# One gate and one lead of a planned order: attention and a feed-forward stage on one core

## The chip, the cores and the metric

The kernel runs on one core of a Trainium2 chip. A core has five engines that run beside each other, each through its own list of instructions: TensorE (PE in the profile, with PEld for its weight loads), VectorE (DVE), ScalarE (ACT), GpSimd (POOL) and SyncE (SP, which here only issues DMAs). They wait for each other by semaphores. The metric is the device time of one execution in microseconds.

## The reference

Eight batches of attention whose 12 heads are mixed twice, and then a feed-forward stage with a squared ReLU:

```python
batch, n_heads, seq, head_dim = (8, 12, 448, 64)
scores = scale * np.matmul(q, k.transpose(0, 1, 3, 2))
scores = np.einsum('bhij,hg->bgij', scores, w_pre)
scores = scores - np.max(scores, axis=-1, keepdims=True)
attn = np.exp(scores)
attn = attn / (np.sum(attn, axis=-1, keepdims=True) + 1e-09)
attn = np.einsum('bhij,hg->bgij', attn, w_post)
return np.matmul(attn, v).astype(np.float32)
...
x = np.ascontiguousarray(attn_out.transpose(0, 2, 1, 3)).reshape(B * S, H * D)
h = np.maximum(x @ w_in, 0.0)          # x: 3584 x 768, w_in: 768 x 2048
return (h * h @ w_out).astype(np.float32)
```

## The kernel before

Batches are counted from 0 to 7. A batch's 448 queries fall into 45 chunks of mostly 10 queries (`NCHUNK`, `CI`), and the chunks into four blocks (`C0 = [0, 6, 19, 32]`). The work of a batch:

- Loads by GpSimd (`load_q`, `load_kv`, `load_tail`): `qs`, `ks`, `vs`, `qt`. Queries and keys come in two halves of six heads.
- Turning queries and keys: in batches 0 and 1 on TensorE against an identity (`t_qk`, L618; `t_tail`, L646); from batch 2 on by copies on GpSimd (`x_piece`, L682) and transposing DMAs on SyncE (L695 for keys, L701 for queries, L665 for the tail).
- `score` (L763): queries times keys, per block. The result is evicted from PSUM to `snat` by VectorE (L556) or ScalarE (L558).
- `relayout` (L794): a DMA on SyncE that gathers a chunk's 10 queries of all 12 heads from `snat` into one tile `sch` of 120 rows. There are 14 `sch` tiles.
- Mixing the heads before the softmax: one matmul with `wmix` (L923), or, for two chunks at once, eight quarter-array matmuls (`mix_two`, L869; 60 or 64 rows and columns). Fourteen chunks of batch 0 take another way, without a relayout (L929).
- The softmax of a chunk: minimum on VectorE (L934), exponential with the sum on ScalarE (L937), the reciprocal of two chunks' sums at once on VectorE (L944), and the scaling of the second mixing weights by these on GpSimd (L947, "weight scaling", one per chunk, so two wait for the same reciprocal).
- The second mixing (L954: four matmuls), eviction to `atb`, and the product with `vs` in half-array matmuls (`av`, L1000), evicted to `xt`.
- The feed-forward stage in units of 128 or 256 columns of `xt` (`unit`): L1059 (`w_in`), ReLU to `hr` on VectorE (L1073) or ScalarE (L1077), square to `h` on GpSimd (L1080), L1098 (`w_out`), eviction to `osb`, store (L1122).

The order in which each engine gets its instructions is not written by hand. A `Planner` gets every operation with its engines, a duration, a rank (`pri`) and what it depends on, runs through them on a clock of its own, and at each moment takes the ready operation of least rank on each engine. What it takes is emitted, in that order; the chip runs these lists as they stand. Rank counts in chunks: chunk `n` of batch `b` has `n = b * NCHUNK + place`. The mix has rank `n`, the weight scaling `n + 0.5`, the second mixing `n + 1.5`; feed-forward work has ranks of a million and more, so it fills what attention leaves. The planner also puts idle filler matmuls (L1323, tile `still`) where it sees TensorE idle in the first 130 us.

What the change touches: `AHEAD` is the lead of a relayout over its chunk,

```python
pri = n - AHEAD                                                                  # L808, relayout
pri = n - o % (2 * PAIRS) + 0.1 * (o % (2 * PAIRS)) - AHEAD                      # L828, in pairs
pri = b * NCHUNK + first - AHEAD - 0.6 - (0.7 if r == 0 else 1.4) * (NPAIR - p)  # L768, score
```

and `Q1_AT` says behind which places of batch 0 the two halves of batch 1's queries and keys are loaded. `load_ahead(1, n, ...)` gives them the rank `n + LATER` (`LATER = 2`), and `gate(n)` makes them depend on the weight scaling of place `n`. The planner lets an operation on the same engine go 70 ns behind a weight scaling's end (`lat=70` at L983).

Of the kernel before, what the change touches and what calls it, by code (L numbers as in the profile page):

```python
# [40 lines left out]
PIECE = NPAIR // 2  # L41
NE = 6
NSCH = 14
AHEAD = 7.5
FIFO = 50
IDLE_NS, IDLE_COLS, IDLE_FROM, IDLE_END, IDLE_LOW = 112, 256, 1300, 130000, 0.62
SPELL, PHASE, DROP, RISE = 3413, 1700, 0.4, 0.8
# [38 lines left out]
NEAR_AT = 5  # L86
SOON = 0
W2_AT = [14, 17, 20, 23]
Q1_AT = [9, 11]
W1_AT = [0, 1, 2, 3, 4, 5]  # L90
W1_GATE = 0
TAIL0, Q0 = 19, 0.7
# [270 lines left out]
def kernel(  # L363
# [370 lines left out]
    def place_of(b, c):  # L734
        return b * NCHUNK + (ORDER0.index(c) if b == 0 else c)
# [6 lines left out]
    def is_direct(b, c):  # L742
        return b == 0 and C0[1] <= c <= C0[2]
# [5 lines left out]
    def score(b, r, group):  # L749
# [17 lines left out]
        first = min(place_of(b, c) for c in range(C0[r], (C0 + [NCHUNK])[r + 1]) if not is_direct(b, c)) - b * NCHUNK  # L767
        pri = b * NCHUNK + first - AHEAD - 0.6 - (0.7 if r == 0 else 1.4) * (NPAIR - p)  # L768
        n = b * (NJ + 1) + r - 2
# [30 lines left out]
    def relayout(b, c):  # L800
# [6 lines left out]
        deps = list(scopy[b, r]) + (list(scopy[b, r - 1]) if r == 1 and cc == 0 else [])  # L807
        pri = n - AHEAD  # L808
        if r == 2 and cc == 0:
# [15 lines left out]
        else:  # L825
            o = cc - 1
            if b >= PAIR_FROM:
                pri = n - o % (2 * PAIRS) + 0.1 * (o % (2 * PAIRS)) - AHEAD  # L828
            o, step = (2 * CI * (o // 2) + o % 2, 2) if b >= PAIR_FROM else (o, CPR)
# [376 lines left out]
    def load_w2(f4, n):  # L1206
        f_, c_ = 8 * (f4 % 2), 384 * (f4 // 2)
        done = load(64, (62, 79), n, lambda: nc.gpsimd.dma_start(
            out=w2[:, f_:f_ + 8, c_:c_ + 384],
            in_=moe_w_out[128 * f_:128 * f_ + 1024, c_:c_ + 384].rearrange("(f p) c -> p f c", p=128),  # L1210
        ), gate(n))
        done.next.append(w2_in[f4])
        w2_in[f4].left += 1
# [8 lines left out]
    def load_ahead(b, n, g0):  # L1222
        wars = [op for p in range(g0 // 2, g0 // 2 + 3) for op in got_op[b - 1, p]]
        got = [
            load(48, (36, 52), n + LATER, lambda: load_q(b, g0, g0 + 6), wars + gate(n)),
            load(42, (46, 58), n + LATER, lambda: load_kv(ks, k, b, g0, g0 + 6), wars + gate(n)),
        ]
        if g0 == 0:
            load_tails(b, n + LATER, got_tail[b - 1] + gate(n))
        later[b, g0] = add("BOTH", 0, n, lambda: None, got, lat=0)  # L1230

    def first_batch():
# [7 lines left out]
        for n, c in enumerate(ORDER0):  # L1240
# [12 lines left out]
            if n in W2_AT:  # L1253
                load_w2(W2_AT.index(n), n)
            if n in Q1_AT:
                load_ahead(1, n, 6 * Q1_AT.index(n))
            if c == C0[1]:
# [106 lines left out]
```

## Time and profile before

| | |
|---|---|
| median of 3 runs | 568.91 us (567.85 to 569.1) |
| the profiled execution | 569.35 us |
| its span in the profile | 567.6 us |
| TensorE busy | 558.4 us, 98% |
| VectorE busy | 500.7 us, 88% |
| ScalarE busy | 446.9 us, 79% |
| GpSimd busy | 363.4 us, 64% |
| read from and written to HBM | 45.61 MB, 11.01 MB |

The span is the profiled execution from its first to its last instruction; the time of the execution is 1.75 us longer. Busy shares are shares of the span. A row of a timeline gives the start in us, the length in us, engine, line, operation, tile written and tiles read, and the number of instructions joined; in brackets stands the idle time before it and what ended it. A matmul's recorded length contains its way through the array, so neighbours overlap, and what one costs is read from start to start.

### The profile page before, as it was taken

What the parts mean: (1) busy time and instruction counts of PE and PEld (TensorE: products, weight loads), DVE (VectorE), ACT (ScalarE), POOL (GpSimd) and SP (SyncE); (2) the same over time, 40 slices, a digit from 0 to 9 for tenths busy, and PEclk for the clock granted to TensorE, in tenths of its full rate; (3) what the DMA queues carried; (4) which work ended last, traced back from release to release, by engine and by line L of the source; (5) the groups of instructions that cost most, each with busy time, mean ns of one, the idle gap of its engine ahead of it and who ended that gap; (6) DMA issues with size and microseconds to landing.
All of it is one profiled execution on the core that took longest, in us unless ns stands there. A gap on an engine that the chain in (4) does not pass through costs nothing.

```text
span 567.6 us, 17890 instructions
## 1 busy us (share of the span) xinstructions
PE 558.4 (98%) x6323; PEld 397.4 (70%) x6323; DVE 500.7 (88%) x1112; ACT 446.9 (79%) x1183; POOL 363.4 (64%) x677
## 2 busy tenths in 40 slices
PE   7999999999999999999999999999999999999997
PEld 4668676786676757677667677767667676767785
DVE  7999999998989999989998998998989999988542
ACT  5788989888769788897898888877878889989200
POOL 9776358676585738857679457957479563746351
PEclk9999999999999999999999999999999999999999
DMA  9999849964999649964699649975399746632011
GB/s 138 211 179 219 163 118 183 203 136 90 151 197 154 152 120 181 193 156 110 102 212 163 162 114 148 201 156 130 73 191 176 136 136 124 143 75 89 1 57 55
DMA packets 129949, 80.85 MB, mean 142 GB/s; under 512 B 59274, under 2 KB 126588, under 8 KB 129860
## 3 DMA queue, kind: packets, MB, share of 16 engines
q1 hardware_dynamic: 80756, 46.29, 37.2%
q0 software_dynamic: 49104, 33.43, 36.4%
q8 instruction: 49, 0.80, 0.6%
q14 instruction: 40, 0.33, 0.2%
HBM read 45.61 MB, written 11.01 MB: 100 GB/s over the span
## 4 chain that ended last, share of the span: by engine, by line
PE 89%; DMA 3%; POOL 2%; DVE 2%; ACT 2%; issue 1%; ACTq 0%; POOLq 0%; DVEq 0%; SPq 0%
PE bank L1098 26%; PE bank L1059 25%; PE bank L954 14%; PE bank L1000 7%; PE bank L763 7%; PE bank L869 5%; PE bank L923 3%; DMA sch<-snat 2%; PE bank L929 1%; DMA qs<-in_q_dram 1%; ACT es L937 1%; POOL wq L947 1%; PE bank L618 1%; DVE osb L912 1%; DVE hr L1073 0%
## 5 line engine op out<-in xcount | busy, mean ns | idle before, releaser
L937 ACT ACTIVATE es<-bank,mn 124x448 bf16<-124x448 f32 (+1 forms) x360 | 228.4, 644 | 30.6 <-DVE mn L934 26.7
L934 DVE TENSOR_REDUCE mn<-bank 124x1 f32<-124x448 f32 (+1 forms) x360 | 209.4, 613 | 5.0 <-PE bank L869 3.7
L1098 PE MATMUL bank<-w,h 128*128 128x384 bf16 (+2 forms) x912 | 179.7, 323 | 0.1
L1059 PE MATMUL bank<-xt,w 128*128 128x256 bf16 (+1 forms) x1632 | 163.9, 254 | 0.5 <-DVE hr L1073 0.2
L1059 PEld LDWEIGHTS <-w 128*128 128x128 bf16 x1632 | 133.5, 98 | 24.2 <-issue 10.3
L947 POOL TENSOR_SCALAR wq<-wback_two,rc 124x120 bf16<-124x120 f32 x252 | 88.7, 363 | 82.0 <-DVE rc L944 56.9
L1080 POOL TENSOR_TENSOR h<-hr 128x512 bf16<-128x512 f32 x112 | 115.9, 1037 | 34.4 <-DVE hr L1073 17.8
L954 PEld LDWEIGHTS <-es 124*112 124x112 bf16 (+2 forms) x1440 | 107.9, 129 | 30.9 <-issue 5.6
L556 DVE CAST atb<-bank 112x480 bf16<-112x480 f32 (+3 forms) x195 | 116.7, 608 | 9.6 <-PE bank L954 8.8
L954 PE MATMUL bank<-wq,es 124*112 124x120 bf16 (+2 forms) x1440 | 120.5, 217 | 1.0 <-POOL wq L947 0.4
L558 ACT CAST atb<-bank 112x480 bf16<-112x480 f32 (+3 forms) x188 | 101.0, 548 | 22.3 <-PE bank L954 20.6
L1098 PEld LDWEIGHTS <-h 128*128 128x128 bf16 x912 | 79.8, 98 | 53.4 <-issue 14.7
L558 ACT CAST snat<-bank 128x448 bf16<-128x448 f32 x169 | 85.2, 543 | 11.9 <-PE bank L763 10.9
L556 DVE CAST snat<-bank 128x448 bf16<-128x448 f32 x149 | 87.7, 614 | 1.7 <-PE bank L763 0.6
L937 ACT ACTIVATION_READ_ACCUMULATOR es<-bank,mn 124x1 f32 (+1 forms) x360 | 75.6, 210 | 0.0
L1073 DVE TENSOR_SCALAR hr<-bank 128x512 f32<-128x512 f32 x83 | 57.1, 688 | 19.3 <-PE bank L1059 15.3
L947 POOL TENSOR_SCALAR wq<-wback,rc 124x120 bf16<-124x120 f32 (+1 forms) x94 | 33.4, 363 | 39.8 <-DVE rc L944 24.7
L763 PE MATMUL bank<-kt,qz 64*64 64x448 bf16 (+1 forms) x528 | 45.8, 362 | 0.1
L869 PE MATMUL bank<-sch,wmix 64*64 64x448 bf16 x504 | 42.7, 361 | 0.4 <-DMA sch<-snat 0.4
L1000 PE MATMUL bank<-atb,vs 112*64 112x192 bf16 (+3 forms) x864 | 40.4, 250 | 0.0
L1122 POOL DMA_DIRECT2D out_dram<-osb x33 | 19.9, 605 | 30.9 <-DVE osb L556 20.5
L1000 PEld LDWEIGHTS <-vs 112*64 112x64 bf16 x864 | 36.4, 110 | 3.6 <-issue 2.4
(80 smaller groups left out, 393.9 us busy)
## 6 DMA issues: line engine op xcount, KB each, us to landing
sch<-snat SPq DMA_DIRECT2D x318, 105.0 KB
out_dram<-osb POOLq DMA_DIRECT2D x21, 384.0 KB, 3.2
vs<-in_v_dram POOLq DMA_DIRECT2D x16, 336.0 KB, 7.9
ks<-in_k_dram POOLq DMA_DIRECT2D x14, 336.0 KB, 8.3
qs<-in_q_dram POOLq DMA_DIRECT2D x14, 288.0 KB, 9.1
w<-in_moe_w_in_dram POOLq DMA_DIRECT2D x6, 512.0 KB, 13.3
w<-in_moe_w_out_dram POOLq DMA_DIRECT2D x4, 768.0 KB, 20.4
out_dram<-osb POOLq DMA_DIRECT2D x8, 192.0 KB, 3.4
```

The lines of the kernel that those rows point to most:

```text
L556: nc.vector.tensor_copy(out=out_, in_=in_)
L558: nc.scalar.copy(out=out_, in_=in_)
L763: nc.tensor.matmul(slot[m0:m1, 0:S], lhsT=lhsT[:, m0:m1], rhs=kt[i][half, :, at_, :], start=True, stop=True,)
L869: nc.tensor.matmul(got[i + x][o0:o1, 0:S], lhsT=w[k0:k1, c0:c0 + o1 - o0], rhs=srcs[i + y][k0:k1, :], start=True, stop=True,)
L934: nc.vector.tensor_reduce(out=mn[i][0:rows, :], in_=slots[mk][0:rows, 0:S], axis=AX.X, op=ALU.min)
L937: nc.scalar.activation(out=es[i][0:rows, 0:S], in_=slots[mk][0:rows, 0:S], func=ACT.Exp, scale=-1.0, bias=mn[i][0:rows, 0:1], accum_out=sm ...
L947: nc.gpsimd.tensor_scalar(out=wq[i][0:rows, :, 0:ns], in0=back[0:rows, :, 0:ns], scalar1=rc[i // 2][0:rows, i % 2:i % 2 + 1], scalar2=1.0, ...
L954: nc.tensor.matmul(slot[0:P_KEYS, jb * H * ns:(jb + 1) * H * ns], lhsT=es[i][0:rows, jb * P_KEYS:(jb + 1) * P_KEYS], rhs=wq[i][0:rows, :, ...
L1000: nc.tensor.matmul(v_[64 * hh:64 * hh + 64, i, 0:x1 - x0], lhsT=vs[:, 2 * c2 + hh, jb, :], rhs=atb[half][:, jb, 2 * c2 + hh, x0:x1], start ...
L1059: nc.tensor.matmul(slot[:, j * w:(j + 1) * w], lhsT=w1[c2][:, (f0 + j) * 128:(f0 + j + 1) * 128], rhs=xt[:, c2, a:z], start=(c2 == 0), sto ...
L1080: nc.gpsimd.tensor_tensor(out=h2_[:, f0:f0 + nf, 0:w], in0=hr[gi % 2][:, :].rearrange("p (f c) -> p f c", f=nf), in1=hr[gi % 2][:, :].rear ...
L1098: nc.tensor.matmul(slot[:, 0:c1 - c0], lhsT=h2_[:, ft, mt * 128:(mt + 1) * 128], rhs=w2[:, ft, c0:c1], start=(ft == 0), stop=(ft == FT - 1),)
```

## The change

Two constants are altered. `AHEAD` goes from 7.5 to 7.4, which gives every relayout and every score a rank that is larger by 0.1. `Q1_AT` goes from places 9 and 11 of batch 0 to 8 and 10: the loads of batch 1's first half depend on the weight scaling of place 8, the first of the pair 8 and 9, and have the rank 10 for 11; those of the second half depend on place 10 and have the rank 12 for 13. No operation is added or taken away; the planner makes its order anew.

```diff
-AHEAD = 7.5
+AHEAD = 7.4
...
-Q1_AT = [9, 11]
+Q1_AT = [8, 10]
```

## The prediction

> **What bounds the kernel now.** I read the page first: span, engine sums, granted clock.
>
> ```profile
> span 567.6 us, 17890 instructions
> PE 558.4 (98%) x6323; PEld 397.4 (70%) x6323; DVE 500.7 (88%) x1112; ACT 446.9 (79%) x1183; POOL 363.4 (64%) x677
> PEclk9999999999999999999999999999999999999999
> ```
>
> TensorE has work in 98% of the span, at the full granted clock throughout. Then the windows view, cut where the stages change (columns: length, busy us of PE, PEld, DVE, ACT and POOL, clock, DMA share, GB/s).
>
> ```profile
> 0.00:40.00 40.00, 36.09 (x298) 23.22 (x299) 36.40 (x110) 28.20 (x70) 31.81 (x63) 1.00 1.10 172
> 40.00:140.00 100.00, 99.29 (x1344) 72.00 (x1346) 94.77 (x211) 87.79 (x239) 63.92 (x121) 1.00 0.87 161
> 140.00:260.00 120.00, 118.82 (x1346) 82.33 (x1336) 111.49 (x242) 100.95 (x271) 80.16 (x153) 1.00 0.85 162
> 260.00:540.00 280.00, 279.74 (x3151) 201.33 (x3149) 248.97 (x537) 229.96 (x607) 177.79 (x332) 1.00 0.66 131
> 540.00:568.00 28.00, 24.40 (x198) 18.50 (x196) 9.04 (x15) 0.00 (x0) 9.75 (x11) 1.00 0.17 57
> ```
>
> Between 40 and 540 us PE is idle for 0.71 + 1.18 + 0.26 = 2.15 us. The other idle time is the start (3.91 us) and the last eviction and store (3.60 us). But busy time joins overlapping records, so I checked against start-to-start distances at the end of the trace:
>
> ```profile
> 516.03 1.48 PE L1059 MATMUL bank<-xt,w 128*128 128x256 bf16 x12
> 517.34 0.58 PE L954 MATMUL bank<-wq,es 124*112 124x120 bf16 x8
> 517.76 1.48 PE L1059 MATMUL bank<-xt,w 128*128 128x256 bf16 x12
> 519.17 0.57 PE L869 MATMUL bank<-sch,wmix 64*64 64x448 bf16 x8
> 519.67 1.49 PE L1059 MATMUL bank<-xt,w 128*128 128x256 bf16 x12
> 530.07 1.47 PE L1098 MATMUL bank<-w,h 128*128 128x384 bf16 x8
> 531.47 2.81 PE L1000 MATMUL bank<-atb,vs 112*64 112x256 bf16 x48
> 534.21 9.27 PE L1098 MATMUL bank<-w,h 128*128 128x384 bf16 x56
> 543.32 10.64 PE L1059 MATMUL bank<-xt,w 128*128 128x256 bf16 x96
> 553.80 10.60 PE L1098 MATMUL bank<-w,h 128*128 128x384 bf16 x80
> ```
>
> Twelve L1059 matmuls take 517.34 - 516.03 = 1.31 us in the mixed stage, 109 ns each; the 96 at the end, beside no attention work, take 553.80 - 543.32 = 10.48 us, 109 ns each too. So the mixed stage runs at the undisturbed rate. The time is PE's work, plus switches of the array's tiling, plus the few waits. The Trainium skill, "Perfetto Trace Analysis", section "Identifying the Most-Contended Engine", says that matmul busy time does not show how close a kernel is to its roofline, and that the share of weight loads does. By that rule PE, at 70%, would have room for a denser order; the equal 109 ns of the two stages speak against it.
>
> **The loads' gate.** The pool's instructions around it in the trace:
>
> ```profile
> 31.64 0.70 POOL L947 TENSOR_SCALAR wq<-wback_far,rc 120x120 bf16<-120x120 f32 x2 [2.14 <-DVE rc L944]
> 32.29 0.88 POOL L411 DMA_DIRECT2D qs<-in_q_dram  x1
> 33.17 0.78 POOL L422 DMA_DIRECT2D ks<-in_k_dram  x1
> 33.94 1.33 POOL L417 DMA_DIRECT2D qt<-in_q_dram  x2
> 36.44 0.87 POOL L411 DMA_DIRECT2D qs<-in_q_dram  x1
> qs<-in_q_dram POOLq DMA_DIRECT2D x14, 288.0 KB, 9.1
> 51.02 0.39 PE L618 MATMUL bank<-ident,ks 112*64 112x112 bf16 x8
> ```
>
> The pair of scalings at 31.64 is places 8 and 9; the loads follow at 32.29. Moving the gate from 9 to 8 would let them off at most half of 0.70 us earlier, 0.35 us. But their rank is 8 + 2 = 10, and the pair's second scaling has rank 9 + 0.5 = 9.5 and waits for the same reciprocal: in the planner's queue it still goes first. The written orders of the two kernels agree: GpSimd's instructions are the same up to the first h after the third weight load, so all six of these loads stand where they stood, and the 48 KB loads and the second group behind the next pair too. On the chip this part gains nothing; were it let off 0.35 us earlier, the first use is at 51.02, 51.02 - 32.29 = 18.7 us after the issue against a landing of 9.1 us. Cost and gain: 0. What it does change is the planner's clock: it counts 70 ns between a scaling and what it lets off, which the loads no longer wait. Every later near-tie in its heaps can turn on that, and from about 38 us on all five engines' orders differ.
>
> **The relayouts' lead, 7.5 to 7.4.** Relayouts and scores rank 0.1 later. A relayout that had the fraction .5 has .6, so the transposing DMAs at .0 and .5 on SyncE win ties, and the times at which these become ready change with the rest. Written orders: of SyncE's 404 rows batch 2's (batches are counted from 0) first key transposition falls behind one relayout and its query transposition behind two; its second key transposition goes ahead of two; the same in the batches behind, a place or two each. A relayout's issue:
>
> ```profile
> 110.09 2.27 SPq L695 DMA_TRANSPOSE kt<-kn  x1
> 113.78 14.26 SPq L794 DMA_DIRECT2D sch<-snat  x14
> 129.58 1.37 SPq L695 DMA_TRANSPOSE kt<-kn  x1
> ```
>
> 14.26 / 14 = 1.02 us each, so two places are 2.0 us for a transposition, and a transposition ahead is 1.37 to 2.27 us for a relayout. What covers it is PE's other work between a score block and its first mix: counted with 109 ns per L1059, 164 per L1098 and so on, at least 5.0 us in the old order (batch 2), 6.5 us at the same place in the new. Cost 0 while that stands; without the cover, the whole 2 us.
>
> **What the reordering costs PE.** Instructions of every real kind are equal in number; the idle filler at L1323 goes from 33 to 34, in time that PE waits anyway: 0. Switches, from the rows at 516 to 534 us: a stretch of quarter-array matmuls costs 519.17 - 517.76 - 1.31 = 0.10 us to enter, and to leave it about 0.50 - 0.37 = 0.13 us (two groups of four at some 0.185 us each, an estimate: 448 columns at 109/256 ns). A half-array stretch costs 1.40 - 8 x 0.164 = 0.09 us to enter and 2.74 - 48 x 0.0545 = 0.12 us to leave. The old order has 125 quarter, 31 half and 10 half-row stretches, the new 124, 33 and 9: sum -1 + 2 - 1 = 0 stretches, 0.0 us. Ten PSUM evictions move from VectorE to ScalarE:
>
> ```profile
> L556 DVE CAST snat<-bank 128x448 bf16<-128x448 f32 x149 | 87.7, 614 | 1.7 <-PE bank L763 0.6 <-PE bank L923 0.2 <-DMA sch<-snat 0.2
> L558 ACT CAST snat<-bank 128x448 bf16<-128x448 f32 x169 | 85.2, 543 | 11.9 <-PE bank L763 10.9 <-DMA sch<-snat 0.4
> ```
>
> That is 10 x 0.61 = 6.1 us off DVE (88%), 5.4 us onto ACT (79%), neither the bound: 0. The end is alike: behind the last half-array stretch PE has 56 L1098 matmuls left in the old order (9.1 us), 50 in the new (8.2 us), against the one xt eviction that the last FFN matmuls wait for (evictions: see the 0.54 to 0.61 us above).
>
> So the terms that can be counted come to 0, and what decides is how many waits the new order meets. A sample of what one costs:
>
> ```profile
> 155.00:160.00 5.00, 4.59 (x39) 3.14 (x38) 3.62 (x7) 2.77 (x9) 3.74 (x6) 1.00 1.28 230
> 157.22 0.67 PE L869 MATMUL bank<-sch,wmix 64*64 64x448 bf16 x4
> 158.08 0.38 PE L869 MATMUL bank<-sch,wmix 64*64 64x448 bf16 x2 [0.19 <-DMA sch<-snat]
> 158.68 0.38 PE L869 MATMUL bank<-sch,wmix 64*60 64x448 bf16 x2 [0.22 <-DMA sch<-snat]
> 158.99 1.26 PE L1059 MATMUL bank<-xt,w 128*128 128x256 bf16 x10
> 147.04 0.90 POOL L411 DMA_DIRECT2D qs<-in_q_dram  x1
> 150.04 1.58 POOL L422 DMA_DIRECT2D vs<-in_v_dram  x2
> ```
>
> Here eight matmuls took 158.99 - 157.22 = 1.77 us where the eight at 519.17 took 0.50: 1.27 us lost, of which the idle column has 0.41. A loss is thus some 3 times the idle time shown, and 40 to 540 us lose about 3 x 2.15 = 6.5 us. The cause is a burst of loads from 147.04 on, with the DMA share at 1.28, beside relayouts. The Trainium skill, "DMA: Bandwidth & Descriptors", section "Issuing engines are not separate DMA queues", says that DMAs of all issuing engines share the same 16 DMA engines and interleave; the row agrees. Batch 3's burst stands behind the same 94 to 95 weight scalings in the new order, so this loss has no reason to go.
>
> A newly drawn order: if all 500 us lost as 140 to 260 did, idle is 500 x 1.18 / 120 = 4.9 us; as 260 to 540 did, 500 x 0.26 / 280 = 0.46 us. The mean is 2.7 us, 0.55 over now, times 3: +1.6 us; I take +1.5. The ends: 3 x 4.9 - 6.5 = +8.2 us and 3 x 0.46 - 6.5 = -5.1 us.
>
> Against its own time the profiled execution (569.35, 1.75 around the span) would come to 570.9. It lies 0.44 above the median of the runs, 568.91; I put the sum there: 570.4 us.
>
> **Rivals.** (1) No change: the gate moves nothing and the ties cancel, 568.9. For it: the equal work and stretches; against it: every engine's order differs from 38 us on. (2) Faster, because the reshuffle thins batch 2's burst:
>
> ```profile
> 93.98 0.78 POOL L422 DMA_DIRECT2D ks<-in_k_dram  x1
> 121.78 1.16 POOL L682 COPY kn<-ks 112x512 bf16<-112x512 bf16 x2
> ```
>
> In the new order the last keys stand seven scalings later, and scores begin with 6.5 instead of 5.0 us in hand; if waits like that at 157 us (1.27) and a smaller one of half a us go, 568.9 - 1.8 = 567.1. It decides where the relayouts land before their mix. (3) The same move starves PE: at 121.78 the copies of those keys run, 27.8 us after their issue. Seven scalings at 500 / 360 = 1.4 us per chunk are 9.7 us, which leaves 18.1 us against a landing of some 9. It would decide only beyond that; then PE waits, and a 3 to 5 us hole gives 572 to 574. I count it in the slower case. The room rule above, were it right, would belong to rival 2.
>
> **How the numbers follow.** A run of this kernel can be told from no change beyond about 0.2% (1.1 us). Slower by more, 0.44 (its own range 570.1 to 574.8); within, 0.30; faster by more, 0.26. Slower leads because at most 6.5 us of loss can go while new waits have no such limit, and the newly drawn mean lies above the present. The range 566.2 to 574.8 leaves out a tenth at either end.
>
> **What would show it.** GpSimd's first loads of batch 1 at 32 and 36 us as now; idle PE between 40 and 540 us from 2.2 to some 2.7 us; the L869 wait near 157 us still there. The forecast is wrong if L869 and L923 no longer wait for sch (time below 567.8), or if one hole above 1 us appears (above 572).

## The result

The changed kernel takes 568.08 us (median; 566.85 to 570.27), the kernel before 569.42 us (567.85 to 571.84) in the same comparison: ratio 0.9974, 95% interval 0.9963 to 0.9986. It became faster by 0.26%; the prediction had 570.4 us and slower. The time lies within the range of the prediction (566.2 to 574.8), on the side that it gave a chance of 0.26. The profiled execution of the changed kernel took 567.65 us with a span of 565.7 us, against 569.35 and 567.6 before.

Page of the changed kernel, span, engine sums and granted clock:

```profile
span 565.7 us, 17927 instructions
PE 557.7 (99%) x6324; PEld 397.6 (70%) x6324; DVE 494.8 (87%) x1102; ACT 450.4 (80%) x1193; POOL 363.7 (64%) x677
PEclk9999999999999999999999999999999999999999
```

Windows of the changed kernel (length, busy us of PE, PEld, DVE, ACT, POOL, clock, DMA share, GB/s):

```profile
0.00:40.00 40.00, 37.73 (x299) 24.21 (x300) 35.46 (x109) 27.78 (x70) 31.75 (x63) 1.00 1.08 171
40.00:140.00 100.00, 98.16 (x1334) 71.00 (x1330) 94.24 (x210) 88.58 (x240) 63.45 (x119) 1.00 0.92 163
140.00:260.00 120.00, 119.43 (x1370) 85.10 (x1369) 111.41 (x244) 102.97 (x276) 82.58 (x159) 1.00 0.87 161
260.00:540.00 280.00, 279.89 (x3145) 199.88 (x3143) 245.18 (x528) 231.05 (x610) 176.47 (x328) 1.00 0.66 133
```

TensorE still bounds the kernel, at the full clock. Its idle time between 40 and 540 us rose from 2.15 to 1.84 + 0.57 + 0.11 = 2.52 us. By that column alone the changed kernel should be slower. So I counted otherwise: each matmul of the trace gets its undisturbed cost (109 ns per 256 columns at full array, a half or a quarter of that in the smaller tilings, 0.1 us per switch of the tiling), and what the real start lies behind the sum of these costs, at the same amount of work done, is time lost. This is an estimate, worked out from all PE rows of each trace:

| PE work done, us | lost before, us | lost after, us |
|---|---|---|
| 0 to 40 (until some 53 us on the clock) | 12.74 | 12.76 |
| 40 to 140 (until 155 to 157 us) | 2.54 | 4.53 |
| 140 to 260 (until some 279 us) | 4.30 | 1.19 |
| 260 to the end | 2.52 | 1.81 |
| sum | 22.10 | 20.29 |

The work itself is equal (542.1 and 542.0 us). How much is lost in all hangs on the costs put in: half a per cent more for each matmul would take 2.7 us off both sums. The difference between the kernels does not hang on them, since both hold the same matmuls. The changed kernel loses 2.0 us more early and gets 3.1 and 0.7 us back later.

The early loss, in the timeline of the changed kernel:

```profile
70.36 0.49 PE L1098 MATMUL bank<-w,h 128*128 128x384 bf16 x2
71.63 0.91 PE L763 MATMUL bank<-kt,qz 64*64 64x448 bf16 x8 [0.77 <-DVE snat L556]
57.29 3.31 SPq L794 DMA_DIRECT2D sch<-snat  x3
70.95 1.16 DVE L556 CAST snat<-bank 128x448 bf16<-128x448 f32 x2 [1.46 <-DMA sch<-snat]
```

The scores wait for a bank. Its eviction on VectorE waits until the relayouts that read the old `snat` have landed; the last of them, the third of the SyncE row, is issued at 59.84 us and lands at 70.87, by the semaphore records of the trace. Two L1098 are 0.33 us of work, so 71.63 - 70.36 - 0.33 = 0.94 us are lost. The kernel before has no such wait. It is the largest single one of the early losses in this trace.

The wait near 157 us, on the other hand, is gone. The timeline of the changed kernel, PE, SyncE (eight relayouts) and GpSimd, and its window:

```profile
154.82 0.38 PE L869 MATMUL bank<-sch,wmix 64*64 64x448 bf16 x4
155.03 0.36 PE L763 MATMUL bank<-kt,qz 64*64 64x448 bf16 x4
155.22 0.36 PE L869 MATMUL bank<-sch,wmix 64*64 64x448 bf16 x4
155.51 0.82 PE L1098 MATMUL bank<-w,h 128*128 128x384 bf16 x4
140.59 6.86 SPq L794 DMA_DIRECT2D sch<-snat  x8
148.27 0.90 POOL L411 DMA_DIRECT2D qs<-in_q_dram  x1
```

```profile
150.00:160.00 10.00, 10.00 (x103) 6.30 (x102) 9.96 (x22) 8.42 (x24) 6.05 (x11) 1.00 1.26 178
```

The same SyncE row and the same window in the kernel before:

```profile
143.35 7.53 SPq L794 DMA_DIRECT2D sch<-snat  x8
```

```profile
150.00:160.00 10.00, 9.59 (x87) 5.78 (x85) 8.62 (x18) 7.40 (x21) 6.06 (x11) 1.00 1.26 196
```

The burst of loads is as thick as before (DMA share 1.26 in both). But the relayouts of the two mixes that waited (by the semaphores that the mixes wait for, the fifth to eighth of this row) were all issued by 140.59 + 6.86 = 147.45, before the burst. In the kernel before the eighth is issued at 150.1, in its middle. PE wants it when the first four matmuls are done, at 157.22 + 0.38 = 157.6, so 7.5 us behind the issue, and gets it 8.6 us behind the issue (158.68).

The second place is at 208 to 213 us. The kernel before:

```profile
209.76 0.42 PE L954 MATMUL bank<-wq,es 124*112 124x120 bf16 x4
210.35 0.42 PE L954 MATMUL bank<-wq,es 124*112 124x120 bf16 x4 [0.16 <-ACT es L937]
210.88 0.54 PE L923 MATMUL bank<-sch,wmix 124*128 124x448 bf16 x2
211.44 0.63 PE L954 MATMUL bank<-wq,es 124*112 124x120 bf16 x8
212.03 0.54 PE L923 MATMUL bank<-sch,wmix 124*128 124x448 bf16 x2
212.61 0.42 PE L954 MATMUL bank<-wq,es 124*112 124x120 bf16 x4
212.96 2.81 PE L1000 MATMUL bank<-atb,vs 112*64 112x256 bf16 x48
```

The changed kernel:

```profile
209.39 0.37 PE L954 MATMUL bank<-wq,es 124*112 124x120 bf16 x4
209.60 0.92 PE L923 MATMUL bank<-sch,wmix 124*128 124x448 bf16 x4
210.35 0.49 PE L1098 MATMUL bank<-w,h 128*128 128x384 bf16 x2
```

Before, mixes and second mixings stand bare, one behind the other. Twenty L954 and four L923 take 212.96 - 209.76 = 3.20 us; undisturbed they are 20 x 0.0525 (the eight of 517.34 took 0.42 us) + 4 x 0.19 (four took 210.35 - 209.60 = 0.75 us) = 1.80 us. So 1.40 us are lost, and the brackets show 0.16 us of it. In the changed kernel feed-forward matmuls stand between, and no such loss is there. Four of the runs below (the loads of batch 1 moved, and the burst at 147 us moved in three ways) leave PE's order as it is in the kernel before; in the trace of each the same 24 matmuls take 3.2 us again. So this loss goes with the order on PE and not with the data of one execution.

### The profile page after: what moved, and what is told of

It reads as the page before. It is cut to its first block, busy times and chain, and to the rows that moved or that the text cites. A ratio compares the mean times of both kernels' runs of the same rounds, so it can differ in the third digit from the quotient of the medians.

```text
span 565.7 us, 17927 instructions
## 1 busy us (share of the span) xinstructions
PE 557.7 (99%) x6324; PEld 397.6 (70%) x6324; DVE 494.8 (87%) x1102; ACT 450.4 (80%) x1193; POOL 363.7 (64%) x677
## 4 chain that ended last, share of the span: by engine, by line
PE 89%; DMA 3%; DVE 3%; ACT 2%; issue 1%; POOL 1%; DVEq 0%; ACTq 0%; POOLq 0%
PE bank L1098 26%; PE bank L1059 24%; PE bank L954 14%; PE bank L1000 7%; PE bank L763 6%; PE bank L869 5%; PE bank L923 3%; DMA sch<-snat 3%; PE bank L929 1%; PE bank L1323 1%; DVE mn L934 1%; DMA kt<-kn 1%; ACT es L937 1%; PE bank L618 1%; DVE hr L1073 1%
## 5 line engine op out<-in xcount | busy, mean ns | idle before, releaser
L1098 PE MATMUL bank<-w,h 128*128 128x384 bf16 (+2 forms) x912 | 179.9, 323 | 0.0
L954 PEld LDWEIGHTS <-es 124*112 124x112 bf16 (+2 forms) x1440 | 109.1, 129 | 30.7 <-issue 6.2
L556 DVE CAST atb<-bank 112x480 bf16<-112x480 f32 (+2 forms) x195 | 117.3, 616 | 8.9 <-PE bank L954 8.3
L954 PE MATMUL bank<-wq,es 124*112 124x120 bf16 (+2 forms) x1440 | 121.1, 217 | 0.6 <-DVE hr L1073 0.3
L1098 PEld LDWEIGHTS <-h 128*128 128x128 bf16 x912 | 79.6, 98 | 51.5 <-issue 13.7
L558 ACT CAST atb<-bank 112x480 bf16<-112x480 f32 (+3 forms) x188 | 98.4, 540 | 21.5 <-PE bank L954 19.4
L558 ACT CAST snat<-bank 128x448 bf16<-128x448 f32 x175 | 88.0, 551 | 10.8 <-PE bank L763 8.9
L556 DVE CAST snat<-bank 128x448 bf16<-128x448 f32 x143 | 84.6, 614 | 3.0 <-DMA sch<-snat 1.7
L1073 DVE TENSOR_SCALAR hr<-bank 128x512 f32<-128x512 f32 x79 | 54.5, 690 | 20.0 <-PE bank L1059 16.9
L763 PE MATMUL bank<-kt,qz 64*64 64x448 bf16 (+1 forms) x528 | 45.6, 360 | 1.6 <-DVE snat L556 0.8
L869 PE MATMUL bank<-sch,wmix 64*64 64x448 bf16 x504 | 41.3, 362 | 0.0
L1000 PE MATMUL bank<-atb,vs 112*64 112x192 bf16 (+3 forms) x864 | 40.6, 250 | 0.0
L1000 PEld LDWEIGHTS <-vs 112*64 112x64 bf16 x864 | 36.6, 110 | 4.9 <-issue 4.3
```

Of the source, the lines that this page charges most:

```text
L556: nc.vector.tensor_copy(out=out_, in_=in_)
L558: nc.scalar.copy(out=out_, in_=in_)
L763: nc.tensor.matmul(slot[m0:m1, 0:S], lhsT=lhsT[:, m0:m1], rhs=kt[i][half, :, at_, :], start=True, stop=True,)
L869: nc.tensor.matmul(got[i + x][o0:o1, 0:S], lhsT=w[k0:k1, c0:c0 + o1 - o0], rhs=srcs[i + y][k0:k1, :], start=True, stop=True,)
L954: nc.tensor.matmul(slot[0:P_KEYS, jb * H * ns:(jb + 1) * H * ns], lhsT=es[i][0:rows, jb * P_KEYS:(jb + 1) * P_KEYS], rhs=wq[i][0:rows, :, ...
L1000: nc.tensor.matmul(v_[64 * hh:64 * hh + 64, i, 0:x1 - x0], lhsT=vs[:, 2 * c2 + hh, jb, :], rhs=atb[half][:, jb, 2 * c2 + hh, x0:x1], start ...
```

## The experiments

The rival theories: (A) the change only makes the planner draw another order, and the time is what waits that order meets; (B) a shorter lead helps by itself; (C) an earlier gate and earlier loads help by themselves; and for the wait at 157 us, that the burst makes it. No kernel here leaves work out.

**Each half alone.** The kernel before with one constant changed:

```diff
-AHEAD = 7.5
+AHEAD = 7.4
```

> Only the relayouts' lead goes to 7.4; the loads' gates stay at places 9 and 11. Its order is the old one up to about 100 us. Theory A (the change only makes the planner draw another order, and the time is the waits which that order meets): between 566.5 and 571 us, with the old order's small losses before 100 us, and its waits near 157 us and 210 us may stay or go. Theory B (the shorter lead itself helps): faster than before by 0.2% or more, and as fast as both edits together (ratio 0.997). Theory C (the earlier loads help): the same as before, ratio 0.999 to 1.001.

Measured 571.82 us against 569.41: ratio 1.0044 (1.0029 to 1.006). Slower, and above the 571 us that theory A allowed.

```diff
-Q1_AT = [9, 11]
+Q1_AT = [8, 10]
```

> Only the gates go to places 8 and 10; the lead stays 7.5. The six loads stand where they stood on GpSimd, but the order differs from about 38 us on. Theory A (another order is drawn): a time of its own, 566.5 to 571 us, not tied to that of both edits. Theory B (the shorter lead helps): the same as before, ratio 0.999 to 1.001. Theory C (the earlier loads help): ratio 0.997, as with both edits.

Measured 571.46 us: ratio 1.0041 (1.0027 to 1.0056). Slower too, and above 571 us as well. Each half alone costs 2 to 2.5 us, both together gain 1.3. The halves do not add, so the gain is not that of either by itself. Their largest waits, from the waits view of the first and of the second, are new ones each:

```profile
PE bank L923 <- DMA sch<-snat: 1.3, 1, 1.3
```

```profile
PE bank L763 <- DMA kt<-kn: 1.4, 1, 1.4
```

**The gate as it was meant.** The order of the kernel before on all engines, but the six loads of batch 1 really moved ahead of the pair's second weight scaling (`placed` moves emitted operations):

```diff
-                load_ahead(1, n, 6 * Q1_AT.index(n))
+                i_ = len(load_ops); load_ahead(1, n, 6 * Q1_AT.index(n)); moves.extend((op, n, 0) for op in load_ops[i_:])
...
-        for op, args in pl.run():
+        for op, args in placed(pl.run(), moves, wq_op):
...
+def placed(order, moves, wq_op):
+    for op, to, behind in moves:
+        item = next(x for x in order if x[0] is op)
+        order.remove(item)
+        order.insert(behind + next(i for i, x in enumerate(order) if x[0] is wq_op[to]), item)
+    return order
```

> The old order, with one thing moved: the six loads of batch 1 stand on GpSimd really ahead of the second weight scaling of their pair (places 9 and 11), as the edit's words have it. Nothing else moves. Theory C (the earlier loads help): faster, ratio 0.997, because keys and queries land up to 0.35 us earlier. Theory A: no gain from the loads (first use 18.7 us behind the issue); the second scaling of each pair waits 3.0 us and 1.7 us behind the issues, so the chunk's second mixing is late: the same or slower by up to 3 us (ratio 1.000 to 1.005).

Measured 573.41 us: ratio 1.0078 (1.006 to 1.0095). The timeline of GpSimd and PE:

```profile
31.70 0.36 POOL L947 TENSOR_SCALAR wq<-wback_far,rc 120x120 bf16<-120x120 f32 x1 [2.14 <-DVE rc L944]
32.12 0.88 POOL L411 DMA_DIRECT2D qs<-in_q_dram  x1
35.11 0.39 POOL L947 TENSOR_SCALAR wq<-wback_far,rc 120x120 bf16<-120x120 f32 x1
35.56 0.37 PE L954 MATMUL bank<-wq,es 120*112 120x120 bf16 x4 [1.70 <-POOL wq L947]
```

The issues run on GpSimd itself, so the second scaling begins 35.11 - 32.06 = 3.05 us behind the end of the first, and PE waits for it. The loss is above the 1.005 that I expected at most. A part of it is the clock of TensorE, which the same trace has at half right behind this wait (window from 37 to 40 us; columns as above):

```profile
37.00:40.00 3.00, 3.00 (x12) 1.35 (x11) 1.97 (x5) 2.39 (x8) 2.08 (x4) 0.50 1.27 172
```

It is at half for 3.4 us in all, from 36.7 us on, which costs about 1.7 us (an estimate: half of the work of that time). Theory C falls: letting the loads off earlier costs, and the changed kernel does not do it.

**The burst at 147 us.** Still the order of the kernel before; on GpSimd alone batch 2's two value loads go behind chunk 100's weight scaling:

```diff
+            ...; b == 1 and moves.extend((op, 100, 1) for op in load_ops[:-3:-1])
```

> The old order, with one thing moved: the two loads of batch 2's values (336 KB each, issued at 150.04 us in the burst) stand behind the weight scaling of chunk 100, some 10 us later on GpSimd. Nothing else moves. If the burst of loads made the relayouts late that TensorE waits for at 157 us, that wait (1.27 us) shrinks to below 0.5 us and the time falls by 0.8 to 1.3 us (ratio 0.998). If the relayouts were late for another reason (their issue on SyncE, the eviction before), the wait at 157 us stays and the ratio is 0.9995 to 1.001.

Measured 569.88 us: ratio 1.0012 (1.0003 to 1.0021). Its timeline on PE at the place:

```profile
157.55 0.59 PE L869 MATMUL bank<-sch,wmix 64*64 64x448 bf16 x6
158.51 0.38 PE L869 MATMUL bank<-sch,wmix 64*60 64x448 bf16 x2 [0.37 <-DMA sch<-snat]
158.82 1.38 PE L1059 MATMUL bank<-xt,w 128*128 128x256 bf16 x11
```

The eight take 158.82 - 157.55 = 1.27 us, so 0.77 us are lost in place of 1.27: less, but not the 0.5 us or below that I expected, and the time did not fall. Then all six loads of the burst behind chunk 100:

```diff
+                    ...; b == 2 and c == 3 and moves.extend((op, 100, 1) for op in load_ops[:i_ - 1:-1])
```

> The old order, with one thing moved: all six loads that GpSimd issues from 147.04 to 151.6 us (batch 3's first queries, keys and tails, batch 2's values) stand behind the weight scaling of chunk 100, some 10 us later. Nothing else moves. If the loads in flight made the relayouts late, the 1.27 us lost at 157 us goes (below 0.3 us) and what follows decides the time: ratio 0.998 if nothing new is late, up to 1.002 if the later burst meets other relayouts, as it did at 172 us in the last run. If the loads had nothing to do with it, the wait at 157 us stays.

Measured 576.79 us: ratio 1.0133 (1.0108 to 1.0158). Its window and its timeline on PE:

```profile
150.00:160.00 10.00, 10.00 (x101) 6.57 (x99) 8.93 (x19) 7.41 (x21) 4.05 (x8) 1.00 0.61 156
```

```profile
157.58 0.57 PE L869 MATMUL bank<-sch,wmix 64*64 64x448 bf16 x8
158.09 1.48 PE L1059 MATMUL bank<-xt,w 128*128 128x256 bf16 x12
167.86 0.56 PE L954 MATMUL bank<-wq,es 124*112 124x120 bf16 x4 [2.66 <-POOL wq L947]
174.35 0.37 PE L954 MATMUL bank<-wq,es 124*112 124x120 bf16 x4 [1.05 <-POOL wq L947]
```

The DMA share falls from 1.26 to 0.61 and the wait is gone: 0.51 us for eight. So the burst did hold up the relayouts, as the prediction said. The Trainium skill, "DMA: Bandwidth & Descriptors", section "Issuing engines are not separate DMA queues", says that DMAs issued by GpSimd and by SyncE run on the same DMA engines; the trace agrees. But the loads put together stand in front of weight scalings, and PE waits there for longer than it did at 157 us. Beside the wait of 2.66 us the granted clock falls to half here too, for 3.4 us from 167.5 on. The time is far above the 1.002 that I expected at most. Spread singly instead (batch 3's first keys behind chunk 97's scaling, batch 2's values behind 99's and 103's):

```diff
+                    ...; b == 2 and c == 3 and moves.append((load_ops[i_ + 1], 97, 1))
+            ...; b == 1 and moves.extend([(load_ops[-2], 99, 1), (load_ops[-1], 103, 1)])
```

> The order of before; on GpSimd alone, batch 3's first keys go behind chunk 97's weight scaling and batch 2's two values one each behind chunk 99's and chunk 103's, so that the burst from 147 us is spread and no more than one issue (0.8 us) stands in front of a scaling. If the burst alone makes the wait near 157 us and single issues on GpSimd are covered: L869 there within 0.8 us for eight matmuls (before 1.77, undisturbed 0.50), no wait of L954 for wq above 0.5 us, ratio 0.998 to 1.000 (0.5 to 1.1 us gained, 568.3 to 568.9). If single issues in front of a scaling cost too: L954 waits for wq, ratio 1.001 to 1.006. If the time given back later, as with the two values moved alone: ratio 1.000 to 1.001 with the wait gone.

Measured 571.41 us: ratio 1.0038 (1.0023 to 1.0054). The gain that I expected did not come. Its timeline on PE:

```profile
156.55 0.57 PE L869 MATMUL bank<-sch,wmix 64*64 64x448 bf16 x8
157.05 1.48 PE L1059 MATMUL bank<-xt,w 128*128 128x256 bf16 x12
171.73 0.38 PE L763 MATMUL bank<-kt,qz 64*64 64x448 bf16 x4 [0.81 <-DVE hr L1073]
180.46 1.18 PE L1000 MATMUL bank<-atb,vs 112*64 112x192 bf16 x24 [1.21 <-DMA vs<-in_v_dram]
```

The wait at 157 us is gone (0.50 us for eight), and two new ones came: the values now land too late for L1000 (1.21 us), and another bank is late. In each of the three runs the time came out above that of the kernel before, though the wait near 157 us was shorter or gone.

**Other draws.** The lead at 7.3, at 7.6, and at 7.45 with the new gates:

> Lead 7.3, gates at 9 and 11. Theory A (each setting draws another order): a time of its own, most likely 1.002 to 1.007 of before, as the two single edits gave 1.0044 and 1.0041. Theory B (a lead that is best near 7.5 and worse on both sides): 1.006 to 1.010, further off than 7.4's 1.0044.

> Lead 7.6, gates at 9 and 11. Theory A: a time of its own, most likely 1.002 to 1.007. Theory B (best near 7.5, smoothly worse on both sides): near 1.004, as 7.4 gave on the other side. A time below 1.000 speaks for A.

> Lead 7.45 with the gates at 8 and 10: half of the lead's step, with the whole step of the gates. If the two edits gain because they fit each other, this lies between the gates alone (1.0041) and both (0.9974): 0.998 to 1.003. Theory A: no such order; anything from 0.997 to 1.008.

Measured 577.94 us (1.0154; 1.0131 to 1.0178), 574.52 us (1.0094; 1.0072 to 1.0117) and 572.71 us (1.006; 1.0036 to 1.0083). The first two are slower than either theory had them. A shorter lead does not help by itself: 7.4 and 7.3 are both slower than 7.5, and theory B of the list above falls. A lead that is best near 7.5 and worse on both sides is not excluded by 7.3, 7.4, 7.5 and 7.6 alone (1.0154, 1.0044, 1 and 1.0094). With the new gates, though, 7.4, 7.45 and 7.5 give 0.9974, 1.006 and 1.0041, which has no order. In the first run a part is again the clock: beside a wait of 2.2 us its trace has it at half for 6.8 us, from 211.9 on, some 3.4 us by the same estimate, and all five executions show a mean clock of 0.991 to 0.994. The lead at 7.4 from batch 2 on, and from batch 3 on (in the three lines of the lead):

```diff
-        pri = n - AHEAD
+        pri = n - (AHEAD if b < 2 else 7.4)
```

> The lead is 7.4 from batch 2 on and 7.5 before; the loads' gates as before. The order on SyncE, GpSimd and VectorE is that of the kernel before up to about batch 2, so nothing before some 140 us can differ. Theory A (every change of the planner's input draws another order, and the time is what waits that order meets): a time of its own between 566.5 and 576 us, most likely 1.000 to 1.010 of the kernel before, and not the 1.0044 of the lead at 7.4 throughout, whose idle before 140 us it shares not at all. Theory B (a shorter lead is better or worse by itself): 1.004, as with 7.4 throughout, since seven... of eight batches' relayouts have it.

> The lead is 7.4 from batch 3 on only. Theory A: a time of its own, 1.000 to 1.010 of the kernel before most likely, bound to neither the time of 7.4 throughout nor that of 7.4 from batch 2 on; the wait of L869 near 157 us is changed or not as the relayouts of that time happen to stand. Theory B (the lead by itself): between 1.000 and 1.004, below that of 7.4 from batch 2 on if that is above 1.

Measured 573.02 us (1.0075; 1.0052 to 1.0099) and 572.91 us (1.0065; 1.0046 to 1.0084). Less of the shorter lead costs no less than the lead at 7.4 throughout (1.0044), as theory A allows and B does not. And a change that means nothing on the chip, one ns in one planned duration:

```diff
-        w = wq_op[n] = add("POOL", 370, n + 0.5, f_wq, ...
+        w = wq_op[n] = add("POOL", 371, n + 0.5, f_wq, ...
```

> The planner is told 371 ns for a weight scaling in place of 370; nothing else is altered, and the change means nothing on the chip, but the written order differs on every engine from some 130 us on. Theory A: the time moves as far as with the constants of the change, by 0.2 to 1.5%, most likely up (1.000 to 1.010; 569 to 575 us). If the constants matter for what they say (an earlier gate, a shorter lead), this one stays at the time of before: 0.999 to 1.001.

Measured 572.88 us: ratio 1.0069 (1.0053 to 1.0085). One of its new waits, in its timeline:

```profile
458.81 0.71 PE L954 MATMUL bank<-wq,es 124*112 124x120 bf16 x8 [0.74 <-POOL wq L947]
```

Two of its executions ran at the full clock and took 572.58 and 572.83 us. This speaks for theory A: another order alone, drawn by a nanosecond, moves the time by 0.69%, more than twice what the change under study did.

**The changed kernel disturbed by one ns**, up (371) and down (369):

> The changed kernel with the planner told 371 ns for a weight scaling in place of 370. PE's order differs from the changed kernel's from about 38 us on. Theory A (the changed kernel is one draw of many, a good one): this one is like other draws, 1.003 to 1.010 of the kernel before (571 to 575 us), the gain gone. If the earlier gate and the shorter lead together are worth something: it keeps 0.996 to 0.999.

> The changed kernel with 369 ns for 370. Theory A: a draw of its own, 1.003 to 1.010 of the kernel before. If the two constants are worth something: 0.996 to 0.999, like the changed kernel.

Up: 568.2 us, ratio 0.998 (0.997 to 0.9991); down: 573.17 us, ratio 1.0065 (1.0049 to 1.008). The first kept the gain, against my expectation, and the written orders tell why: with buffer numbers left out, it differs from the changed kernel by one mix moved past one second mixing and one square moved on GpSimd, and SyncE, VectorE and ScalarE have the same order. It is the same draw. The second has another order on PE from the 301st of 6324 matmuls on, and the gain is gone. The same order gives the same time, another order another.

**The burst put back into the changed kernel**, on GpSimd alone (the traces show the first load 3.1 and 4.0 us earlier):

```diff
+                    ...; b == 2 and c == 3 and moves.extend((op, 91, 1) for op in load_ops[:i_ - 1:-1])
+            ...; b == 1 and moves.extend((op, 94, 1) for op in load_ops[:-3:-1])
```

> The order of the changed kernel; on GpSimd alone, the first loads of batch 3 (queries, keys, the two tail loads) go from behind chunk 94's weight scaling to behind chunk 91's, some 2.5 us earlier, and batch 2's two values to behind chunk 94's. In the kernel before these loads began 3.7 us behind the first of the fourteen relayouts in question (143.35 to 147.04), in the changed kernel 7.7 us (140.59 to 148.27); here some 5. If the distance of loads and relayouts decides the wait that the changed kernel is rid of: mixes (L869, L923) between 150 and 160 us wait for sch again, 0.3 to 1.3 us, and the time goes up by about that: ratio to the kernel before 0.998 to 1.000. If the wait went for another reason: no wait for sch, ratio 0.997 to 0.998, or more only by waits of L954 for wq, behind the four issues (3 us) that now stand in front of three scalings.

> As the run beside it, with the first loads of batch 3 behind chunk 89's scaling, some 4.5 us earlier than in the changed kernel and 3 us behind the first of the relayouts, the distance of the kernel before (3.7 us). If the distance decides: the wait of the mixes for sch is as in the kernel before, 1 to 1.3 us, ratio 0.999 to 1.001. If not: none, and only waits of L954 for wq (0 to 3 us, ratio 0.997 to 1.003).

Measured 568.97 us (0.9986; 0.9973 to 0.9998) and 568.42 us (0.9986; 0.9975 to 0.9997). The timeline of the second of them (89 for 91):

```profile
141.58 7.41 SPq L794 DMA_DIRECT2D sch<-snat  x8
144.30 0.91 POOL L411 DMA_DIRECT2D qs<-in_q_dram  x1
156.02 0.36 PE L869 MATMUL bank<-sch,wmix 64*64 64x448 bf16 x4
156.31 0.82 PE L1098 MATMUL bank<-w,h 128*128 128x384 bf16 x4
110.69 0.38 PE L869 MATMUL bank<-sch,wmix 64*60 64x448 bf16 x2 [0.88 <-DMA sch<-snat]
```

The loads begin 2.7 us behind the first relayout, closer than in the kernel before (147.04 - 143.35 = 3.7 us), and the mixes near 156 us still don't wait. So the distance of burst and relayouts alone does not make the wait; my theory of it falls. The semaphore records of the traces tell what does. For the eighth relayout of that row: when it is issued, how long it takes to land, and how long behind its issue PE wants it, all in us.

| kernel | issued | lands after | wanted after | PE waits |
|---|---|---|---|---|
| before | 150.1 | 8.5 | 7.5 | yes |
| before, values behind chunk 100 | 151.2 | 7.3 | 6.6 | yes |
| before, all six loads behind chunk 100 | 150.7 | 2.7 | 7.1 | no |
| before, loads spread | 149.7 | 5.9 | 7.0 | no |
| changed | 146.7 | 4.4 | 8.5 | no |
| changed, burst behind chunk 91 | 146.3 | 7.8 | 9.0 | no |
| changed, burst behind chunk 89 | 148.2 | 7.2 | 7.8 | no |

PE waits where the landing takes longer than the lead over the mix, and only there. Without the loads a relayout lands in 2.7 us, beside them in up to 8.5. The changed kernel has both on its side: its eighth relayout is issued 1.6 us ahead of the burst (148.27) and lands early, and its lead is 1.0 us longer. With the burst put back the landing is slow again, and the longer lead covers it. This is read from seven traces; the lead was not varied by itself.

The last row of the timeline is a wait at a place where the order up to there is that of the changed kernel, whose profiled execution shows no idle time there. That relayout took 10.3 us to land here and 9.2 us there. The loss near 71 us differs too: 0.94 us in the changed kernel's trace, 0.22 and 0.32 us in these two, with the same order up to there.

## Why the prediction was wrong

- *What bounds the kernel*: right. PE's work is the same, the clock is full in both traces, and the time moved only by what PE loses between matmuls. The 3.60 us given for the end were read from a window that goes 0.4 us past the span (567.6); this enters no sum.
- *The loads' gate*: right. In the changed kernel they stand where they stood:

```profile
31.77 0.70 POOL L947 TENSOR_SCALAR wq<-wback_far,rc 120x120 bf16<-120x120 f32 x2 [2.15 <-DVE rc L944]
32.41 0.88 POOL L411 DMA_DIRECT2D qs<-in_q_dram  x1
36.55 0.87 POOL L411 DMA_DIRECT2D qs<-in_q_dram  x1
```

That they would gain nothing if they did move was too kind: the 18.7 us in hand were counted, the scaling queued behind them on GpSimd was not, and the run that moved them lost 0.78%.
- *The lead*: cost 0, "while that stands", held in the changed kernel: no wait for `kt` in it. It did not hold in the kernel with the new gates and the old lead, where L763 waited 1.4 us for `kt`.
- *PE's ledger* (switches, filler, evictions): right; VectorE went from 500.7 to 494.8 us, ScalarE from 446.9 to 450.4, and neither mattered.
- *The wait at 157 us*: the step that failed first. "Batch 3's burst stands behind the same 94 to 95 weight scalings in the new order, so this loss has no reason to go" looked at the loads alone. Their place among the scalings and their density did stay; the relayouts moved. The first of the row stands 3.7 us ahead of the burst before and 7.7 us after, the eighth 3.1 us behind its start before and 1.6 us ahead of it after, and the 1.27 us went. The burst as its cause was right: with the loads moved away or spread the wait is gone, in two runs. What was missing is the comparison of the relayouts' landing, 8.5 us before and 4.4 us after, with their lead over the mix.
- *A loss is 3 times the idle time shown*: failed. Idle time went as forecast, from 2.15 to 2.52 us (2.7 was named), and the time lost behind the first 40 us of work went the other way, from 9.36 to 7.53 us. By the estimate of the table the factor is 9.36 / 2.15 = 4.4 in one kernel and 7.53 / 2.52 = 3.0 in the other; a stretch like 209.76 to 212.96 loses 1.40 us with 0.16 us idle. A sum scaled from the idle column cannot tell the sign of half a per cent.
- *The newly drawn order, +1.5 us*: mis-sized. Of the nine other orders tried (lead 7.3, 7.4, 7.6, 7.45 with the gates, 7.4 from batch 2 and 3, the gates alone, the two one-ns draws that changed the order) all were slower, by 0.41 to 1.54%, mean 0.74% or 4.2 us (in the slowest, lead 7.3, some 3.4 us of the 8.9 are the clock). So "slower" was the right bet for a draw, and should have been larger; the changed kernel is the one of ten that came out below, by 1.3 us, and that it was this one was the luck of the draw. The mean of two stretches says nothing of which waits a new order meets.
- *Rivals*: by the change that it gives, rival 2 came nearest (1.8 us faster, the waits at 157 us go; measured 1.3), and its deciding condition, that the relayouts land before their mix, is what is seen. Its reason, a thinner burst of batch 2, is not: the DMA share of 40 to 140 us rose from 0.87 to 0.92, and at 157 us it is 1.26 in both. Rival 3 did not occur. Rival 1's argument against itself stands.

What stays open: why bare mixes and second mixings lose 1.40 us at 208 us. The loss comes with the order on PE, but no run changed that place alone. The waits of the other orders were read as the largest of each trace, and not traced to the rank that made them. No kernel tried beats the changed one; the one with 371 ns is the same draw (568.2 us).

## What to carry to other kernels

When a planner makes the order anew from nearly equal ranks, a change of a constant is a new draw: ask first whether the constant moves what it names, and if not, price the draw by a few redraws that mean nothing, such as one ns in a duration, before any meaning is read into a gain or a loss of half a per cent. The waits of two orders are compared at equal work done, start against start, not by the idle column. Whether a DMA makes an engine wait takes two numbers, the lead of its issue over its use and the time to its landing beside the other traffic of that moment; the distance to a burst alone does not tell. A DMA issue is work on the engine that issues it, so moving a load is priced by what queues behind it there, even where its landing has 18 us to spare.

## What was not expected of the hardware

Seven-tenths to nine-tenths of a us per load issue on GpSimd stop the compute instructions queued there: four issues in 3.0 us cost PE a wait of 1.70 us at once. And identical orders do not meet identical waits: a relayout that is in time in one execution made PE wait 0.88 us in another kernel with the same order up to there. Last, a long wait can be paid twice: in the three traces with a wait of PE of 1.7 us or more behind the first 20 us (1.70, 2.2 and 2.66 us) the granted clock falls to half beside it, for 3.4 to 6.8 us; in the others, with waits of at most 1.6 us there, it stays full until PE's work is done. No run tried the two apart.
